# Seven-product block pairs of a fused attention and two-MLP kernel: the next pair's operands made in place, and results turned by VectorE

## The chip, the cores and the metric

The kernel runs on one core of one Trainium2 chip. The metric is the device time of one execution in microseconds; before the change it was 1601.54 us, the median of 3 runs (1599.88 to 1603.52).

## The reference

```python
q_s = softmax(q, axis=-1); k_s = softmax(k, axis=2)      # 8 batches, 8 heads, 576 x 64
kv = einsum('bhsd,bhse->bhde', k_s, v)
x = einsum('bhsd,bhde->bhse', q_s, kv)                   # then 4608 tokens x 512
h = x @ w_in;   x = (h * clip(h + 3, 0, 6) / 6) @ w_out  # first MLP, 512 -> 2048 -> 512
h = x @ w2_in;  out = (h * sigmoid(h)) @ w2_out          # second MLP, same sizes
```

All of it is float32, and the output is 4608 x 512. The softmaxes subtract the largest value and add 1e-9 to the sum.

## The kernel before, in words

The 4608 tokens are 9 blocks of 512. Within the program activations lie transposed: a tile has 128 features on the partitions and 512 tokens along the free dimension. Every float32 product is made of three passes of TensorE over rounded halves, high x high, high x low and low x high, so each operand is kept as a high part (a rounding copy on ScalarE) and a low part (a subtraction on VectorE).

`first_block` and `middle` do the attention and the first MLP of blocks 0 to 6, up to about 725 us. `second_mlp` (line 1315) does the rest in five passes and a tail. A pass (`PASSES`, line 56) takes two neighbouring blocks j and j + 1 of one MLP: (second MLP, 1 and 2), (first MLP, 7 and 8), then the second MLP of 3 and 4, 5 and 6, 7 and 8. The tail does the second MLP of block 0 in the ordinary way, hidden block by hidden block.

In a pass the product of the weight's four quarters with the pair's four quarters is made of seven products in place of eight (Winograd's form): sums of quarters of the weights (A11, S1, ...) lie ready in DRAM (`ws`), sums of the pair's quarters (B11, B21, B22, T1 to T4; the dictionary `op`) lie in SBUF, each with a high and a low half and two chunks c. The first half of a pass (`inner`, line 1337, into the hidden layer) has 8 groups of 7 products, the second (`outer`, line 1508, out of the hidden layer) 7 products of 8 steps. A product is 6 matmuls of 128x512. In the first half ScalarE, VectorE and GpSimd join the products and apply the gate (`pair_events`, line 1373); in the second they split the gated tiles, `LOOK` = 4 products ahead (`split`, `split_low`, lines 1449 to 1455), into one of five buffers (`split_tile`), and join the results into the eight tiles `fixed` (`joins`, line 1522).

The order is written by hand: `when(t, fn)` puts a piece of work at time t, counted in products, and the program is issued in the order of t. Each engine then runs its own instructions in that order and waits at the head of its queue for whatever it needs. SP issues all transfers of the passes. Among them are the weights: a ring of six entries, each two slots of `ws` and 512 KB (`fetch`, line 1190); an entry is fetched again as soon as TensorE has read it.

Two pieces of that order concern the change:

- *The next pair's operands* (`x_ahead`, line 1466). In the first half of a pass, four raw tiles per chunk c are loaded, GpSimd makes the differences (`total`), ScalarE the high parts (`high`) and VectorE the low parts (`low`). They go into buffers of `split_tile` and from there to a DRAM tensor `xd`, since the operands' own tiles `op` are still being read by this half. In the second half `x_fetch` (line 1505) brings them back from `xd` into `op`.
- *The results of a second-MLP pass* (`turn`, line 1553). `fixed` holds them transposed. Eight times per pass TensorE transposes four 128x128 blocks into a PSUM bank, ScalarE copies the bank into a small tile, and SP stores it, 256 KB in rows of 2 KB. For passes 1, 3 and 4 this lies in the first half of the pass that follows, for the last pass in the first eight hidden blocks of the tail.

Of the kernel before, what the change touches and what calls it, by code (L numbers as in the profile page):

```python
# [18 lines left out]
P = 128  # L19
# [9 lines left out]
def efficient_attention_then_two_mlps(  # L29
# [54 lines left out]
    xd = dram.tile([7, P, 2, 2, BLK], F32, name="xd")  # L84
# [1230 lines left out]
    def second_mlp(last):  # L1315
# [148 lines left out]
        XS = ("B11", "T2", "T1", "B21", "T3", "B22", "T4")  # L1464

        def x_ahead(b, c, t, step):

            ph, j = PASSES[b]
            st, hl = {}, {}

            def load(n):
                if n in ("B22", "B21"):
                    pair = gs.tile([P, 2, BLK], F32, tag="g", name="xst")
                    st[n], st[{"B22": "B12", "B21": "B11"}[n]] = pair[:, 0], pair[:, 1]
                jj, h = int(n[2] == "2"), int(n[1] == "2")
                nc.sync.dma_start(st[n], yd[j + jj, 2 * h + c] if ph else xq[j + jj - FAR, 2 * h + c])

            def high(n, src):
                hl[n] = split_tile(True)
                nc.scalar.copy(hl[n][0], st[src])  # L1480

            def low(n, src):
                hi, lo = hl.pop(n)
                add(lo, st[src], f32(hi), ALU.subtract)
                to = xd[XS.index(n)]
                nc.sync.dma_start(to[:, 0, c], f32(hi))
                nc.sync.dma_start(to[:, 1, c], f32(lo))
# [16 lines left out]

        def x_fetch(n, low):
            nc.sync.dma_start(f32(op[n][low]), xd[XS.index(n)][:, low])

# [14 lines left out]
        def joins(b, p, t):  # L1522

            def do(m, name):
                one, two, three, four = fixed[4 * m : 4 * m + 4]
                at = d[b, p][m]
                if name in ("s1", "s5", "C11"):
                    nc.scalar.copy({"s1": one, "s5": three, "C11": four}[name], at)
                elif name == "U2":
                    add(two, at, one)  # L1530
                elif name == "U3":
                    d[b, "U3", m] = small("U3")
                    add(d[b, "U3", m], at, one)
                elif name == "C22":
                    add(three, d.pop((b, "U3", m)), three)
                elif name == "C12":
                    add(two, at, two)
                else:
                    add(one, at, one)
# [13 lines left out]
        def turn(j, k, bank=bank):  # L1553

            h, i = (1, k) if k < NCH else (0, k - NCH)
            at = bank()
            for a in range(2):
                for m in range(2):
                    x = fixed[4 * m + ((3, 1), (0, 2))[a][h]]
                    c = 2 * a + m  # L1560
                    nc.tensor.transpose(  # L1561
                        at[:, c * P : (c + 1) * P], x[:, i * P : (i + 1) * P], ident
                    )
            o = small("o2")
            nc.scalar.copy(o, at)
            rows = out[(j + h) * BLK : (j + h + 1) * BLK, :].rearrange("(p i) d -> i p d", i=NCH)
            nc.sync.dma_start(rows[i], o)
# [4 lines left out]
        for b, (ph, j) in enumerate(PASSES):  # L1572
# [35 lines left out]
            if b + 1 < BB:  # L1608
                x_ahead(b + 1, 0, t0 + (7.0 if b else 9.5), 3.0 if b else 2.8)
                x_ahead(b + 1, 1, t0 + 28.0, 3.0)  # L1610
                for m, n in enumerate(XS):
                    for low in range(2):
                        when(
                            start[0] + 3.1 + 6.0 * m + 3.0 * low,
                            lambda n=n, low=low: x_fetch(n, low),
                        )
                for k in range(2 * NCH if ph else 0):
                    when(T + 3.95 + 5.0 * k, lambda j=j, k=k: turn(j, k))
# [23 lines left out]
        for f in range(NF):  # L1642
            s = (1, 0, f)
            mm1(s)
            if f < 2 * NCH:
                turn(PASSES[-1][1], f, a_pool)
# [63 lines left out]
```

## Time and profile before

| what | value |
|---|---|
| runs, median (lowest to highest) | 1601.54 us (1599.88 to 1603.52) |
| profiled execution: own time; span of its instructions | 1602.64 us; 1600.9 us |
| TensorE busy | 1573.0 us, 98% |
| VectorE, ScalarE, GpSimd busy | 1119.9 us (70%), 788.7 us (49%), 473.6 us (30%) |
| granted TensorE clock, mean | 0.998 of full speed |
| DMA | 401.60 MB, mean 251 GB/s, SP's queue 75.1% of the engines' time |

PE is TensorE's matmuls, PEld its weight loads, which run beside them; DVE is VectorE, ACT ScalarE, POOL GpSimd, SP the engine that issues transfers. A row of the chain gives start, length and work; a row of a timeline adds the idle time before the work and what ended it. The rows sit in the section before the prediction.

### The profile page before, as it was taken

What the parts mean: (1) busy time and instruction counts of PE and PEld (TensorE: products, weight loads), DVE (VectorE), ACT (ScalarE), POOL (GpSimd) and SP (SyncE); (2) the same over time, 40 slices, a digit from 0 to 9 for tenths busy, and PEclk for the clock granted to TensorE, in tenths of its full rate; (3) what the DMA queues carried; (4) which work ended last, traced back from release to release, by engine and by line L of the source; (5) the groups of instructions that cost most, each with busy time, mean ns of one, the idle gap of its engine ahead of it and who ended that gap; (6) DMA issues with size and microseconds to landing.
All of it is one profiled execution on the core that took longest, in us unless ns stands there. A gap on an engine that the chain in (4) does not pass through costs nothing.

```text
span 1600.9 us, 23136 instructions
## 1 busy us (share of the span) xinstructions
PE 1573.0 (98%) x7516; PEld 1287.1 (80%) x7516; DVE 1119.9 (70%) x1856; ACT 788.7 (49%) x1422; POOL 473.6 (30%) x443
## 2 busy tenths in 40 slices
PE   5999999999999999999999999999999999999998
PEld 3778888887878888887888888888888888888887
DVE  8898577777767777676877667668757775567522
ACT  5787345455555554454554445444535553445322
POOL 3334133335333334542410451045005500330000
PEclk9999999999999999999999999999999999999999
DMA  9814976777777776758988898898979896669730
GB/s 274 322 37 151 323 200 200 219 219 223 234 218 207 227 232 187 244 171 315 351 298 286 298 349 300 316 318 311 330 255 330 321 330 237 214 227 358 246 126 27
DMA packets 352424, 401.60 MB, mean 251 GB/s; under 512 B 120496, under 2 KB 233136, under 8 KB 352304
## 3 DMA queue, kind: packets, MB, share of 16 engines
q1 hardware_dynamic: 350256, 399.05, 75.1%
q8 instruction: 60, 0.98, 0.3%
q10 hardware_dynamic: 2048, 1.08, 0.2%
q14 instruction: 60, 0.49, 0.1%
HBM read 276.56 MB, written 123.47 MB: 250 GB/s over the span
## 4 chain that ended last, share of the span: by engine, by line
PE 90%; DVE 4%; DMA 3%; ACT 1%; issue 1%; SPq 0%; POOL 0%; ACTq 0%; DVEq 0%; POOLq 0%
PE pb L1516 24%; PE pb L1346 22%; PE h L562 20%; PE y L634 17%; PE y L636 3%; PE pa L516 2%; PE pa L398 1%; PE pb L1561 1%; DVE fa L140 1%; DMA xst<-yd 0%; DVE fa L144 0%; DMA xst<-xq 0%; DVE h L599 0%; DMA yd<-o 0%; DMA ring<-ws 0%
## 5 line engine op out<-in xcount | busy, mean ns | idle before, releaser
L1346 PE MATMUL pb<-xo,ring 128*128 128x512 f32 x1680 | 391.3, 391 | 1.2 <-ACT s L1386 0.9
L562 PE MATMUL h<-x,wi 128*128 128x512 f32 x1536 | 382.8, 396 | 1.8 <-ACT g L610 1.4
L1516 PE MATMUL pb<-gsp,ring 128*128 128x512 f32 x1680 | 382.4, 389 | 0.0
L1516 PEld LDWEIGHTS pb<-gsp,ring 128*128 128x128 f32 x1680 | 315.3, 188 | 65.5
L1346 PEld LDWEIGHTS pb<-xo,ring 128*128 128x128 f32 x1680 | 313.1, 188 | 68.0 <-ACT s L1386 2.9
L562 PEld LDWEIGHTS h<-x,wi 128*128 128x128 f32 x1536 | 285.4, 190 | 63.9 <-ACT g L610 2.2
L634 PE MATMUL y<-g,wo 128*128 128x512 f32 x1344 | 324.6, 391 | 1.1 <-DVE o L653 1.1
L634 PEld LDWEIGHTS y<-g,wo 128*128 128x128 f32 x1344 | 251.1, 188 | 54.1 <-DVE o L653 1.6
L1333 DVE TENSOR_TENSOR gsp<-g,gsp 128x512 fp32r<-128x512 f32 x240 | 171.8, 722 | 72.6 <-ACT gsp L1451 69.4
L1451 ACT CAST gsp<-g 128x512 fp32r<-128x512 f32 x240 | 144.3, 622 | 139.8 <-DVE gsp L1333 70.8
L1333 POOL TENSOR_TENSOR s<-U,s 128x512 f32<-128x512 f32 x32 | 44.3, 1383 | 384.9 <-DVE U L1333 369.4
L575 ACT ACTIVATE r<-h 128x512 f32<-128x512 f32 x112 | 67.0, 598 | 168.0 <-PE h L562 166.3
L599 DVE SCALAR_TENSOR_TENSOR h<-r,h 128x512 f32<-128x512 f32 x112 | 77.5, 692 | 80.4 <-ACT r L575 79.8
L1333 DVE TENSOR_TENSOR g<-r,pb 128x512 f32<-128x512 f32 x96 | 65.5, 683 | 47.9 <-ACT r L1360 47.7
L1360 ACT ACTIVATE r<-pb 128x512 f32<-128x512 f32 x96 | 57.2, 595 | 70.3 <-DVE pb L1333 59.6
L590 ACT CAST g<-h 128x512 fp32r<-128x512 f32 x112 | 65.6, 585 | 48.5 <-DVE h L599 40.8
L437 POOL TENSOR_TENSOR qe<-qraw,qm 128x512 f32<-128x512 f32 x34 | 39.8, 1170 | 153.5 <-DVE qz L479 144.5
L1333 POOL TENSOR_TENSOR g<-g 128x512 f32<-128x512 f32 x40 | 55.3, 1383 | 91.7 <-DVE g L1333 79.8
L593 DVE TENSOR_TENSOR g<-h,g 128x512 fp32r<-128x512 f32 x96 | 66.0, 687 | 20.5 <-ACT g L590 19.0
L195 POOL TENSOR_TENSOR fa<-fa 128x256 f32<-128x256 f32 x64 | 49.6, 774 | 56.8 <-DVE sp L227 48.0
L1333 DVE TENSOR_TENSOR U<-pb,s 128x512 f32<-128x512 f32 x80 | 54.7, 684 | 13.4 <-PE pb L1346 8.4
L1333 DVE TENSOR_TENSOR gsp<-xst,gsp 128x512 fp32r<-128x512 f32 x56 | 54.0, 965 | 12.7 <-ACT gsp L1480 10.9
(167 smaller groups left out, 1829.7 us busy)
## 6 DMA issues: line engine op xcount, KB each, us to landing
ring<-ws SPq DMA_DIRECT2D x280, 512.0 KB, 5.1
ws<-sp SPq DMA_DIRECT2D x256, 128.0 KB, 2.2
xd<-gsp SPq DMA_DIRECT2D x112, 256.0 KB, 5.5
xo<-xd SPq DMA_DIRECT2D x56, 512.0 KB, 6.3
wi_early<-in_moe_w_in_dram SPq DMA_DIRECT2D x16, 512.0 KB, 8.6
wo_early<-in_moe_w_out_dram SPq DMA_DIRECT2D x16, 512.0 KB, 8.8
wi_raw<-in_moe_w_in_dram SPq DMA_DIRECT2D x16, 512.0 KB, 4.8
ws<-w_sum SPq DMA_DIRECT2D x64, 128.0 KB, 2.1
```

The costliest lines, as they stand in the source:

```text
L195: lambda to=to, x=x, y=y, op=op: nc.gpsimd.tensor_tensor(out=at[to], in0=at[x], in1=at[y], op=op)
L562: nc.tensor.matmul(h, w[:, a, c, :], x[:, e, c, :], start=(c == 0 and n == 0), stop=(c == NC - 1 and n == 2),)
L575: nc.scalar.activation(self.r, self.h, AF.Relu, bias=3.0)
L590: nc.scalar.copy(self.g[:, 0], self.r)
L593: nc.vector.tensor_tensor(out=self.g[:, 1], in0=self.r, in1=f32(self.g[:, 0]), op=ALU.subtract)
L599: nc.vector.scalar_tensor_tensor(out=self.h, in0=self.r, scalar=6.0, in1=self.h, op0=ALU.min, op1=ALU.mult)
L634: nc.tensor.matmul(y[c], w[:, a, cs], g[:, e, :], start=st, stop=sp)
L1333: (eng or nc.vector).tensor_tensor(out=out, in0=a, in1=b, op=how)
L1346: nc.tensor.matmul(to, ws_[:, a], e[:, c], start=p in ("P1", "P6", "P5") and c == 0 and m == 0, stop=c == 1 and m == 2, skip_group_check=True,
L1360: nc.scalar.activation(r, d[b, n, key], AF.Sigmoid)
L1451: nc.scalar.copy(t[0], source(p, i))
L1516: nc.tensor.matmul(d[b, p][m], w[:, a, m * P : (m + 1) * P], t[e], start=new and i == 0 and k == 0, stop=i == NPR - 1 and k == 2, skip_gro ...
```

## The change

The scratch tensor `xd` and `x_fetch` are removed. `x_ahead` now runs in the second half of a pass, when the operands' tiles are no longer read, for chunk 0 from slot 6 and for chunk 1 from slot 30 of the half, and writes `op` directly; its raw tiles come from the pool of small tiles. The joins' tile U3 moves to another pool. `turn` is replaced: VectorE's transpose turns 32x32 blocks within a 128x512 tile, and the rest of the transposition is left to the store, four transfers of 64 KB for each tile, in runs of 32 elements (128 B). In the passes these transfers are 1.3 slots apart (`turn_blocks`), in the tail together (`turn_last`).

```diff
-    xd = dram.tile([7, P, 2, 2, BLK], F32, name="xd")
...
             def load(n):
-                if n in ("B22", "B21"):
-                    pair = gs.tile([P, 2, BLK], F32, tag="g", name="xst")
-                    st[n], st[{"B22": "B12", "B21": "B11"}[n]] = pair[:, 0], pair[:, 1]
+                st[n] = small("xst")
...
             def high(n, src):
-                hl[n] = split_tile(True)
-                nc.scalar.copy(hl[n][0], st[src])
+                nc.scalar.copy(op[n][0][:, c], st[src])

             def low(n, src):
-                hi, lo = hl.pop(n)
-                add(lo, st[src], f32(hi), ALU.subtract)
-                to = xd[XS.index(n)]
-                nc.sync.dma_start(to[:, 0, c], f32(hi))
-                nc.sync.dma_start(to[:, 1, c], f32(lo))
+                hi, lo = op[n]
+                add(lo[:, c], st[src], f32(hi[:, c]), ALU.subtract)
...
-        def x_fetch(n, low):
-            nc.sync.dma_start(f32(op[n][low]), xd[XS.index(n)][:, low])
...
-                    d[b, "U3", m] = small("U3")
+                    d[b, "U3", m] = att.tile([P, BLK], F32, tag="q", bufs=2, name="U3")
...
-        def turn(j, k, bank=bank):
-
-            h, i = (1, k) if k < NCH else (0, k - NCH)
-            at = bank()
-            for a in range(2):
-                for m in range(2):
-                    x = fixed[4 * m + ((3, 1), (0, 2))[a][h]]
-                    c = 2 * a + m
-                    nc.tensor.transpose(
-                        at[:, c * P : (c + 1) * P], x[:, i * P : (i + 1) * P], ident
-                    )
-            o = small("o2")
-            nc.scalar.copy(o, at)
-            rows = out[(j + h) * BLK : (j + h + 1) * BLK, :].rearrange("(p i) d -> i p d", i=NCH)
-            nc.sync.dma_start(rows[i], o)
+        turned = []
+
+        def turn_blocks(j, k, part):
+            h, n = (1, k) if k < NC else (0, k - NC)
+            a, m = divmod(n, 2)
+            x = fixed[4 * m + ((3, 1), (0, 2))[a][h]]
+            if part == 0:
+                if not turned:
+                    turned.extend(split_tile())
+                nc.vector.transpose(f32(turned[0]), x)
+            o = f32(turned[0])
+            rows = out[(j + h) * BLK : (j + h + 1) * BLK, n * P : (n + 1) * P]
+            e = slice(part * 32, part * 32 + 32)
+            nc.sync.dma_start(
+                rows[:, e].rearrange("(b r i) c -> r i b c", b=4, i=NCH),
+                o[e].rearrange("r (i b c) -> r i b c", i=NCH, b=4),
+            )
+            if part == 3:
+                turned.pop(0)
+
+        gone = []
+
+        def turn_last(j, k):
...
+            o = gone.pop() if k else small("o2")
+            gone.append(x)
+            nc.vector.transpose(o, x)
...
             if b + 1 < BB:
-                x_ahead(b + 1, 0, t0 + (7.0 if b else 9.5), 3.0 if b else 2.8)
-                x_ahead(b + 1, 1, t0 + 28.0, 3.0)
-                for m, n in enumerate(XS):
-                    for low in range(2):
+                for c in range(2):
+                    x_ahead(b + 1, c, start[0] + (6.0, 30.0)[c], 3.0)
+                for k in range(2 * NCH if ph else 0):
+                    for i in range(4):
                         when(
-                            start[0] + 3.1 + 6.0 * m + 3.0 * low,
-                            lambda n=n, low=low: x_fetch(n, low),
+                            T + 3.95 + 5.8 * k + 1.3 * i,
+                            lambda j=j, k=k, i=i: turn_blocks(j, k, i),
                         )
-                for k in range(2 * NCH if ph else 0):
-                    when(T + 3.95 + 5.0 * k, lambda j=j, k=k: turn(j, k))
...
             if f < 2 * NCH:
-                turn(PASSES[-1][1], f, a_pool)
+                turn_last(PASSES[-1][1], f)
```

VectorE's order moves in the second half of a pass. Here is a piece of the second pass's second half before; `gsp<-g` and `gsp<-spare` are low parts for the products, `g_...<-spare` sums of gated tiles:

```order
L1333 TENSOR_TENSOR gsp<-g_8265,gsp 128x512
L1333 TENSOR_TENSOR gsp<-g_8350,gsp 128x512
L1333 TENSOR_TENSOR gsp<-spare,gsp 128x512
L1333 TENSOR_TENSOR g_7896<-spare,g_7896 128x512
L1333 TENSOR_TENSOR gsp<-spare,gsp 128x512 x2
L1333 TENSOR_TENSOR g_7992<-spare,g_7992 128x512
L1333 TENSOR_TENSOR gsp<-spare,gsp 128x512 x3
L1333 TENSOR_TENSOR g_8087<-spare,g_8087 128x512
```

And the same piece with the change; `xo<-xst` is a low part of an operand of the next pair, made from the raw tile `xst`:

```order
L1332 TENSOR_TENSOR gsp<-g_8249,gsp 128x512
L1332 TENSOR_TENSOR xo<-xst,xo 128x512
L1332 TENSOR_TENSOR gsp<-spare,gsp 128x512
L1332 TENSOR_TENSOR g_7866<-spare,g_7866 128x512
L1332 TENSOR_TENSOR gsp<-spare,gsp 128x512 x2
L1332 TENSOR_TENSOR xo<-xst,xo 128x512
L1332 TENSOR_TENSOR g_7941<-spare,g_7941 128x512
L1332 TENSOR_TENSOR gsp<-spare,gsp 128x512 x3
L1332 TENSOR_TENSOR xo<-xst,xo 128x512
L1332 TENSOR_TENSOR g_8017<-spare,g_8017 128x512
```

The subtractions for the operands now stand between the sums and the low parts for the products, one for about every three products.

SP's order moves in the first half of a pass. Here is a piece of the fourth pass's first half before: raw tiles, weight fetches, the stores to `xd` and one store of a result among them:

```order
L1476 DMA xst<-yd 128x512 x4
L1567 DMA out_dram<-o_11695 128x512
L1193 DMA ring<-ws 128x2x512 x2
L1486 DMA xd<-gsp 128x512
L1487 DMA xd<-gsp 128x512
L1193 DMA ring<-ws 128x2x512
L1567 DMA out_dram<-o_11764 128x512
L1193 DMA ring<-ws 128x2x512
L1486 DMA xd<-gsp 128x512
L1487 DMA xd<-gsp 128x512
```

And with the change, from the third pass's second half into the fourth's first:

```order
L1471 DMA xst<-yd 128x512 x4
L1192 DMA ring<-ws 128x2x512 x17
L1556 DMA out_dram<-gsp 128x4x32
L1192 DMA ring<-ws 128x2x512
L1556 DMA out_dram<-gsp 128x4x32
L1192 DMA ring<-ws 128x2x512
L1556 DMA out_dram<-gsp 128x4x32 x2
L1192 DMA ring<-ws 128x2x512
L1556 DMA out_dram<-gsp 128x4x32
```

The raw tiles are now loaded in the second half, and the first half's queue holds weight fetches and the short stores alone.

TensorE's order loses the transposes. In the fourth pass's first half it had:

```order
L1346 MATMUL pb<-xo,ring 128x512 x30
L1561 MATMUL pb<-ident,vbuf 128x128
L1561 MATMUL pb<-ident,fin 128x128
L1561 MATMUL pb<-ident,kbuf_101 128x128
L1561 MATMUL pb<-ident,fin 128x128
L1346 MATMUL pb<-xo,ring 128x512 x30
```

With the change that half, with the second half before it and the products that lead over into its own, reads:

```order
L1345 MATMUL pb<-xo,ring 128x512 x6
L1504 MATMUL pb<-gsp,ring 128x512 x330
L1345 MATMUL pb<-xo,ring 128x512 x330
L1504 MATMUL pb<-gsp,ring 128x512 x6
L1345 MATMUL pb<-xo,ring 128x512 x6
```

Nothing stands between the products any more.

## Rows read from the trace of the kernel before

**Rows 1.** The page: busy time, share of the span and instructions of each engine.
```profile
PE 1573.0 (98%) x7516; PEld 1287.1 (80%) x7516; DVE 1119.9 (70%) x1856; ACT 788.7 (49%) x1422; POOL 473.6 (30%) x443
```

**Rows 2.** Waits of PE, 720 to 1510 us: who waited for whom; total, times, longest.
```profile
PE pb L1346 <- ACT s L1386: 0.9, 1, 0.9
PE pb L1346 <- DVE U L1333: 0.2, 1, 0.2
```

**Rows 3.** Busy time by stretch: first half, second half, last pass's first half.
```profile
core 0: us, PE busy (x) PEld busy (x) DVE busy (x) ACT busy (x) POOL busy (x), PEclk, DMA share, GB/s
...
1193.10:1269.60 76.50, 76.50 (x354) 63.20 (x353) 53.85 (x74) 36.25 (x68) 39.87 (x29) 1.00 0.94 331
1274.60:1349.40 74.80, 74.80 (x332) 61.94 (x331) 53.28 (x82) 35.12 (x61) 3.30 (x2) 1.00 0.83 295
1349.40:1425.80 76.40, 76.40 (x354) 63.12 (x353) 40.29 (x60) 29.67 (x54) 27.14 (x21) 1.00 0.64 209
```

**Rows 4.** The chain that ended last: first half, second half, tail; start, us, what.
```profile
1199.03 6.86 PE pb L1346 x30
...
1206.32 6.86 PE pb L1346 x30
...
1274.61 74.80 PE pb L1516 x330
...
1514.83 2.72 PE h L562 x12
...
1520.76 2.72 PE h L562 x12
```

**Rows 5.** DMA issues: out<-in, queue, op, count, KB each, median us to landing.
```profile
ring<-ws SPq DMA_DIRECT2D x280, 512.0 KB, 5.1
...
xd<-gsp SPq DMA_DIRECT2D x112, 256.0 KB, 5.5
xo<-xd SPq DMA_DIRECT2D x56, 512.0 KB, 6.3
...
out_dram<-o SPq DMA_DIRECT2D x32, 256.0 KB, 3.7
```

**Rows 6.** Busy time by stretch: the tail, after its last turn.
```profile
1555.00:1590.00 35.00, 35.00 (x156) 28.97 (x155) 8.97 (x13) 7.47 (x13) 0.00 (x0) 1.00 0.06 20
```

**Rows 7.** The chain that ended last, in the first pass's first half.
```profile
740.70 6.83 DMA xst<-xq
...
755.76 0.48 ACT s L1386
```

**Rows 8.** Groups of instructions: line, engine, op, shapes, count; busy us, mean ns; idle before.
```profile
L1333 DVE TENSOR_TENSOR gsp<-xst,gsp 128x512 fp32r<-128x512 f32 x56 | 54.0, 965 | 12.7 <-ACT gsp L1480 10.9 <-DMA xd<-gsp 0.9 <-DMA ring<-ws 0.9
...
L1480 ACT CAST gsp<-xst 128x512 fp32r<-128x512 f32 x56 | 35.0, 626 | 9.8 <-issue 3.0 <-DMA xst<-xq 2.9 <-DMA xst<-yd 2.7
...
L479 DVE STREAM_TRANSPOSE qz<-qe 128x512 f32<-128x512 f32 x27 | 19.0, 705 | 2.2 <-POOL qe L463 0.9 <-DMA yd<-o 0.6 <-DMA ws<-fa 0.5
```

**Rows 9.** Timeline of DVE in the third pass's second half.
```profile
1159.84 0.69 DVE L1333 TENSOR_TENSOR gsp<-g,gsp 128x512 fp32r<-128x512 f32 x1
...
1174.05 0.69 DVE L1333 TENSOR_TENSOR g<-g,spare 128x512 f32<-128x512 f32 x1
1174.65 0.69 DVE L1333 TENSOR_TENSOR kbuf<-U,kbuf 128x512 f32<-128x512 f32 x1
```

**Rows 10.** Timeline of DVE in the fourth pass's first half, GpSimd busy beside it.
```profile
1217.03 1.52 DVE L1333 TENSOR_TENSOR gsp<-xst,gsp 128x512 fp32r<-128x512 f32 x1
```

**Rows 11.** Timeline of ACT in the third pass's second half.
```profile
1159.18 0.62 ACT L1451 CAST gsp<-g 128x512 fp32r<-128x512 f32 x1 [0.74 <-DVE gsp L1333]
```

**Rows 12.** The q loads' issues on SP: duration ns min/median/max, first and last start.
```profile
L489 SPq DMA_DIRECT2D qt<-zd x108: 557/635/1460, 200.7 to 692.1; - x108
```

**Rows 13.** Timeline of SP in the third pass's second half.
```profile
1122.46 0.36 SPq L1193 DMA_DIRECT2D ring<-ws  x1
...
1125.18 3.08 SPq L1193 DMA_DIRECT2D ring<-ws  x2
```

**Rows 14.** Busy time by stretch: two us in which q loads (issued 310.8 to 313.5) move.
```profile
313.00:315.00 2.00, 2.00 (x11) 1.65 (x10) 1.12 (x4) 0.52 (x2) 1.04 (x1) 1.00 0.63 99
```

More of the change, by code (lines that the diff above doesn't have):

```diff
@@ L1462, in next_t4 @@
             add(g_of(2 * i)[:, 1], g_of(2 * i + 1)[:, 0], op["spare"][:, i], ALU.subtract)
-        XS = ("B11", "T2", "T1", "B21", "T3", "B22", "T4")
         def x_ahead(b, c, t, step):
             ph, j = PASSES[b]
-            st, hl = {}, {}
+            st = {}
             def load(n):
-                if n in ("B22", "B21"):
-                    pair = gs.tile([P, 2, BLK], F32, tag="g", name="xst")
-                    st[n], st[{"B22": "B12", "B21": "B11"}[n]] = pair[:, 0], pair[:, 1]
+                st[n] = small("xst")
                 jj, h = int(n[2] == "2"), int(n[1] == "2")
@@ L1551, in joins @@
                 when(t + k, lambda m=m, name=name: do(m, name))
-        def turn(j, k, bank=bank):
-            h, i = (1, k) if k < NCH else (0, k - NCH)
-            at = bank()
-            for a in range(2):
-                for m in range(2):
-                    x = fixed[4 * m + ((3, 1), (0, 2))[a][h]]
-                    c = 2 * a + m
-                    nc.tensor.transpose(
-                        at[:, c * P : (c + 1) * P], x[:, i * P : (i + 1) * P], ident
-                    )
-            o = small("o2")
-            nc.scalar.copy(o, at)
-            rows = out[(j + h) * BLK : (j + h + 1) * BLK, :].rearrange("(p i) d -> i p d", i=NCH)
-            nc.sync.dma_start(rows[i], o)
+        turned = []
[18 more added lines that the diff above has]
+        def turn_last(j, k):
+            h, n = (1, k) if k < NC else (0, k - NC)
+            a, m = divmod(n, 2)
+            x = fixed[4 * m + ((3, 1), (0, 2))[a][h]]
+            o = gone.pop() if k else small("o2")
+            gone.append(x)
+            nc.vector.transpose(o, x)
+            rows = out[(j + h) * BLK : (j + h + 1) * BLK, n * P : (n + 1) * P]
+            for i in range(4):
+                e = slice(i * 32, i * 32 + 32)
+                nc.sync.dma_start(
+                    rows[:, e].rearrange("(b r i) c -> r i b c", b=4, i=NCH),
+                    o[e].rearrange("r (i b c) -> r i b c", i=NCH, b=4),
+                )
         T = 0.0
@@ L1608, in second_mlp @@
             if b + 1 < BB:
-                x_ahead(b + 1, 0, t0 + (7.0 if b else 9.5), 3.0 if b else 2.8)
-                x_ahead(b + 1, 1, t0 + 28.0, 3.0)
-                for m, n in enumerate(XS):
-                    for low in range(2):
+                for c in range(2):
+                    x_ahead(b + 1, c, start[0] + (6.0, 30.0)[c], 3.0)
+                for k in range(2 * NCH if ph else 0):
+                    for i in range(4):
                         when(
-                            start[0] + 3.1 + 6.0 * m + 3.0 * low,
-                            lambda n=n, low=low: x_fetch(n, low),
-                        )
-                for k in range(2 * NCH if ph else 0):
-                    when(T + 3.95 + 5.0 * k, lambda j=j, k=k: turn(j, k))
+                            T + 3.95 + 5.8 * k + 1.3 * i,
+                            lambda j=j, k=k, i=i: turn_blocks(j, k, i),
+                        )
             else:
```

## Prediction

> **What bounds the kernel now.** I began with the shares of busy time: TensorE is busy for 1573.0 of a 1600.9 us span, VectorE for 1119.9, ScalarE for 788.7 [rows 1]. So time goes where TensorE's instructions go, unless something makes it wait. The waits of TensorE over the five passes say that nearly nothing does: 0.9 us and 0.2 us in some 780 us [rows 2]. The table by stretches shows it stage by stage: in a first half with turns, in a second half, and in the first half of the last pass PE is busy for the whole stretch, 76.50 of 76.50, 74.80 of 74.80 and 76.40 of 76.40 us, at a granted clock of 1.00, that is 2.4 GHz [rows 3]. What the change does to VectorE, GpSimd or the transfers is therefore worth nothing by itself; it counts what it takes from PE's queue, and it costs what it makes PE wait.
>
> **What it takes from PE.** The chain of waits gives the price of a turn. In the second half 330 matmuls take 74.80 us, so one takes 0.2267 us and thirty take 6.80. In the first half thirty matmuls and one turn take 1206.32 - 1199.03 = 7.29 us: a turn (four transposes) costs 0.49 us of PE's time. In the tail twenty-four matmuls and a turn take 1520.76 - 1514.83 = 5.93 us, against 24 x 0.2267 = 5.44: again 0.49 [rows 4]. There are 32 turns, one for each store of a result of 256 KB [rows 5]. The change removes them all: 32 x 0.49 = **15.7 us**. Does PE then run on through the gaps? In the tail from the ninth hidden block on there is no turn already, and there PE is busy for 35.00 of 35.00 us [rows 6]; in the first half of the last pass, after its turns, it is the same [rows 3]. So the turns cover nothing that would show up.
>
> **The wait that goes with them.** The 0.9 us wait is for a copy of line 1386, and the chain has that copy at 755.76 us, in the first pass's first half. Ahead of it the chain holds a transfer of 6.83 us that brings raw operands of the next pair [rows 7]: ScalarE's queue stood behind it, and the gate of the hidden layer behind that. This work leaves the first half. Between 0 and 1.1 us come back; I take 0.9, the whole of that wait, since the cause is gone.
>
> **What moves into the second half.** Per pass but the last, 14 splits of the next pair's operands: a copy on ScalarE (626 ns) and a subtraction on VectorE (965 ns on average, 56 of each in all) [rows 8]. Their 112 stores of 256 KB and the 56 loads of 512 KB go altogether [rows 5], each a place in SP's queue ahead of the weights. The second half leaves DVE 74.80 - 53.28 = 21.5 us and ACT 39.7 us of idle time [rows 3]; 14 x 0.965 = 13.5 us and 14 x 0.626 = 8.8 us fit as a sum. But both queues run in order, so I also count where they are densest. Instructions of DVE follow each other at 0.60 us (1174.65 - 1174.05) [rows 9]. Between the slots 29.7 and 50 of the half (20.3 products of six matmuls, 1.36 us each, 27.6 us) DVE gets 20 splits of products, 8 sums of gated tiles, 7 splits of operands and 6 joins: 41 x 0.60 = 24.6 us. Four GpSimd subtractions fall there too; beside one, a subtraction of VectorE took 1.52 us in place of 0.69 [rows 10], so up to 4 x 0.8 = 3.2 us more: 27.8, as much as there is. What covers the excess is the look-ahead: the copy for a product is made four products early (5.44 us), and copy and subtraction are over 1.35 us after the copy's start [rows 9, 11], so 4.1 us are in hand. Lower bound 0; upper bound, with every DVE instruction at its listed 0.69 us and the lows at 1.52: 34 x 0.69 + 7 x 1.52 = 34.1 us, 6.5 over, 2.4 beyond what is in hand, in each of four halves: 9.6 us. I take **0**, since the 0.60 is read in that very half. The raw operands must land before the first copy, 4.3 slots or 5.8 us after their issue; the slowest landing shown is 6.83 [rows 7], a delay of 1 us, inside the 4.1. On SP the loads stand between weight fetches and wait only for buffers last used in the first half or 4 slots earlier.
>
> **What the turns become.** On VectorE 32 transposes of 128x512. The one transpose that the trace shows took 705 ns [rows 8]; 24 of them fall in first halves, where 14 of the 965 ns subtractions leave and 8 transposes come, so DVE there gets lighter: 53.85 - 13.5 + 8 x 0.71 = 46 of 76.5 us [rows 3, 8]. Cost 0; with GpSimd beside each, 8 x 0.8 = 6.4 us of DVE time, still less than leaves. ScalarE loses 24 + 8 copies. On SP four stores follow each transpose: 128 in all, each 64 KB in 512 runs of 128 B. The nearest issue is that of the q loads, also 64 KB in such runs: 0.635 us [rows 12]. With 28 weight fetches of 0.36 us, SP issues for 32 x 0.635 + 28 x 0.36 = 30 of 76 us. SP waits for a transpose before its first store, and behind that stands a weight fetch. Fetches have room: one follows another at 2.72 us, the ring holds six, so five intervals (13.6 us) pass before use, of which landing takes 5.1 [rows 5, 13]: 8.5 us in hand.
>
> **The transfers themselves** are the open price; no store in short runs to DRAM is in the trace. The q loads' reads are the nearest: about 2 us behind their issue (the usual landing is 2.7) the 16 DMA engines were busy for 0.63 of the time at 99 GB/s [rows 14], which is 48 runs of 128 B per us and engine, 13 ns each. A store then takes 32 x 13 = 0.42 us of each engine, and stores come every 1.3 slots, 1.77 us: share 0.24. The weights' share is that of the last pass's first half, 0.64 at 209 GB/s, less its eight stores: 0.56 [rows 3]. Together 0.80: no queue grows. From the other side, a 2 KB run costs 0.83 of a us for 9 runs per engine, 92 ns [rows 3]; at that price the stores alone would take 94 us of a half of 76. I take 13 ns, the same run length. The Trainium skill ("DMA: Bandwidth & Descriptors", Specifications) states that below 512 B the DMA does a read-modify-write. Taken as twice the price of a run, that would make the share 1.04 and the last store some 2 us late, inside the 8.5 us in hand, and the time 1585 as well; only a costlier round trip for each run leads to rival 2, on whose side the rule stands. No run here shows it yet.
>
> **The sum.** The profiled execution took 1602.64 us, 1.7 beyond its span. 1602.64 - 15.7 - 0.9 = 1586.0. It stood 1.1 above the median of the runs, 1601.54, so the median should come to **1585.0**.
>
> **Rivals.**
> 1. *The second half starves* (0.06). A copy of an operand stands at the head of ScalarE's queue until its transfer or GpSimd's subtraction is there, and copies for the products wait behind it. It decides once a delay passes 4.1 us. Against it: a slowest landing of 6.83 us; for it: DVE's densest 27 us hold 27.8 us of work. If each of four halves loses 3.5 us: 1585 + 14 = 1599, the gain given back.
> 2. *The short stores clog the DMA queues* (0.07), and weight fetches, which share those queues, come late. Every 1.77 us the engines owe 0.99 to the weights; a run at 24 ns fills the rest, and from 38 ns on (15 us late by the last store, less the 8.5 in hand, in three halves) the gain is lost. At four times the read's price, 52 ns: 32 x 0.88 = 28 us late, 20 us of stall in each of three halves: 1585 + 58 = 1643, **slower**. Against it: the reads at 13 ns, a third of the price that decides. For it: a store is not a read, no row shows one, and the bounds reach from 13 to 92 ns.
> 3. *The first half's gate comes late* (0.04): a transpose beside GpSimd sits ahead of a gate's multiplication and holds a PSUM bank. At 2 us in each of three halves: 1591. Against it: VectorE's queue there loses more than it gets.
> 4. *The turns were covered* (0.03): PE then waits where they stood, and the time stays at 1601. Against it: [rows 6].
>
> **Chances and range.** The forecast has 0.80, with a spread of 1581 to 1589 (a single run of before differs from its median by up to 2 us, and the wait's and the second half's bounds are inside). Rival 3 lies within 1592; left out are rivals 1, 2 and 4, together 0.16: range 1581 to 1592. 0.2% is 3.2 us, about what a measurement tells from no change. Faster by more than that: 0.80 + 0.04 and half of rival 1, 0.87; within: the other half and rival 4, 0.06; slower: 0.07.
>
> **What would show it.** Right: no transpose left in PE's list but those of the attention; first halves of the passes all 76.2 us long (336 matmuls); PE's waits over the passes under 1 us; the second halves at 74.8 with DVE near 66 us busy; the store's landing under 4 us, weight fetches still near 5. Wrong: a PE wait for DVE or ACT on gsp in second halves (rival 1), a PE wait for the ring with a DMA share near 1 in the second, fourth and fifth first halves (rival 2), PE waits for g or banks there (rival 3).

## The result, and the profile after

| | before | after |
|---|---|---|
| runs, median (lowest to highest) | 1600.71 us (1599.39 to 1603.52), 4 runs | 1584.31 us (1583.04 to 1585.70), 4 runs |
| ratio after to before, 95% interval | | 0.9895 [0.9878, 0.9913] |
| profiled execution: own time; span | 1602.64 us; 1600.9 us | 1584.67 us; 1583.0 us |

The kernel is faster by 16.4 us; 1585.0 had been forecast. (The median of before is here over four runs, one more than at the time of the prediction.)

The page's busy times, against [rows 1]: PE has 128 matmul records fewer, the four transposes of each of 32 turns, and 17.7 us less work. VectorE has more to do, ScalarE less.

```profile
PE 1555.3 (98%) x7388; PEld 1274.9 (81%) x7388; DVE 1146.3 (72%) x1888; ACT 775.1 (49%) x1390; POOL 490.8 (31%) x443
```

The table of PE's waits between 720 and 1510 us, which had two entries [rows 2], is empty. The chain that ended last is a chain of matmuls alone there (start, us, what); the pieces left out are like these:

```profile
726.28 2.73 PE pb L1345 x12
...
806.54 74.80 PE pb L1504 x330
881.34 74.80 PE pb L1345 x330
...
958.86 74.80 PE pb L1504 x330
...
1490.62 5.44 PE h L561 x24
```

Every half but the very first, which begins among the last products of the stage before, is now 330 matmuls in 74.80 us, with 2.72 us for the twelve that lead over from a first half into a second; the second halves had this length already [rows 4]. The stretches (columns as in [rows 3]) show what lies beside it. In order: a first half with stores, one without, the fourth pass's second half with the new work in it (the three passes before have DVE at 66.47 to 67.08 us there), and 40 us of the densest stores.

```profile
881.30:956.10 74.80, 74.80 (x332) 61.94 (x331) 46.81 (x71) 27.27 (x49) 27.11 (x21) 1.00 0.81 219
1033.70:1108.50 74.80, 74.80 (x331) 61.94 (x330) 42.21 (x63) 27.27 (x49) 27.11 (x21) 1.00 0.60 198
...
1263.50:1338.30 74.80, 74.80 (x331) 61.94 (x331) 66.41 (x95) 42.05 (x75) 21.82 (x10) 1.00 0.66 225
900.00:940.00 40.00, 40.00 (x178) 33.14 (x177) 25.88 (x40) 14.83 (x27) 15.52 (x13) 1.00 0.86 231
```

PE is busy for all of every stretch at a granted clock of 1.00. DVE stands at 66.41 us of 74.80 in the second half, where it had 53.28. The 32 stores of a first half raise the DMA share from 0.60 to 0.81: 0.21 x 74.8 us for 1024 runs of 128 B per engine, 15 ns a run.

The list of DMA issues (out<-in, queue, count, KB each, median us to landing) answers to [rows 5]: over the whole run weight fetches land sooner than before (5.1), the short stores of the passes in 4.0 us.

```profile
ring<-ws SPq DMA_DIRECT2D x280, 512.0 KB, 3.9
...
out_dram<-gsp SPq DMA_DIRECT2D x96, 64.0 KB, 4.0
```

Their issue on SP takes what the q loads' did [rows 12] (view of one line: duration ns min/median/max, first and last start):

```profile
L1556 SPq DMA_DIRECT2D out_dram<-gsp x96: 596/597/1478, 885.5 to 1404.0; - x96
```

Three groups of instructions of after (columns as in [rows 8]). The moved subtraction has become shorter, 681 ns for 965. GpSimd's differences, which were 1382 ns on average in the first halves, have become longer. The transposes cost what the one of [rows 8] did.

```profile
L1332 DVE TENSOR_TENSOR xo<-xst,xo 128x512 fp32r<-128x512 f32 x56 | 38.1, 681 | 5.2 <-ACT xo L1474 4.6 <-DMA ring<-ws 0.3
...
L1552 DVE STREAM_TRANSPOSE gsp<-fin 128x512 f32<-128x512 f32 x12 | 8.5, 704 | 0.0
...
L1332 POOL TENSOR_TENSOR xst<-xst 128x512 f32<-128x512 f32 x32 | 71.5, 2235 | 167.5 <-DVE xo L1332 87.1 <-DMA xst<-yd 46.4 <-DMA xst<-xq 17.3
```

### The profile page after: what moved, and what is told of

Read it like the earlier page. It is cut to its first block, busy times and chain, and to the rows that moved or that the text cites. A ratio compares the mean times of both kernels' runs of the same rounds, so it can differ in the third digit from the quotient of the medians.

```text
span 1583.0 us, 22655 instructions
## 1 busy us (share of the span) xinstructions
PE 1555.3 (98%) x7388; PEld 1274.9 (81%) x7388; DVE 1146.3 (72%) x1888; ACT 775.1 (49%) x1390; POOL 490.8 (31%) x443
## 4 chain that ended last, share of the span: by engine, by line
PE 93%; DVE 3%; DMA 1%; ACT 1%; issue 1%; SPq 0%; POOL 0%; ACTq 0%; DVEq 0%; POOLq 0%
PE pb L1345 24%; PE pb L1504 24%; PE h L561 21%; PE y L633 17%; PE y L635 3%; PE pa L515 2%; PE pa L397 1%; DVE fa L139 1%; DMA yd<-o 0%; DVE fa L143 0%; DVE fa L132 0%; DVE h L598 0%; DMA wi_early<-in_moe_w_in_dram 0%; DMA ws<-fa 0%; PE pa L368 0%
## 5 line engine op out<-in xcount | busy, mean ns | idle before, releaser
L1345 PE MATMUL pb<-xo,ring 128*128 128x512 f32 x1680 | 382.6, 389 | 0.0
L1332 DVE TENSOR_TENSOR gsp<-g,gsp 128x512 fp32r<-128x512 f32 x240 | 182.5, 780 | 25.4 <-ACT gsp L1450 24.7
L1332 POOL TENSOR_TENSOR xst<-xst 128x512 f32<-128x512 f32 x32 | 71.5, 2235 | 167.5 <-DVE xo L1332 87.1
```

What stands on the lines that cost most here:

```text
L1332: (eng or nc.vector).tensor_tensor(out=out, in0=a, in1=b, op=how)
L1345: nc.tensor.matmul(to, ws_[:, a], e[:, c], start=p in ("P1", "P6", "P5") and c == 0 and m == 0, stop=c == 1 and m == 2, skip_group_check=True,
```

## The experiments

Eleven kernels ran, in three groups, each group on one chip together with the kernel before; ratios are to that kernel in the same group (medians 1601.33, 1600.28 and 1600.48 us). The theory is that of the prediction: only what leaves PE's queue counts, the rest is covered. The rivals are the second half that starves (1) and the short stores that delay the weights (2).

### The two parts alone

**In place only.** The change, with the turns as they were (TensorE, a copy on ScalarE, one store of 256 KB):

```diff
-                    for i in range(4):
-                        when(T + 3.95 + 5.8 * k + 1.3 * i,
-                            lambda j=j, k=k, i=i: turn_blocks(j, k, i))
+                    when(T + 3.95 + 5.0 * k, lambda j=j, k=k: turn(j, k))
```

> The kernel with the change, but results are turned as before (TensorE, ScalarE copy, 256 KB stores); only the next pair's operands are made in place in the second half. Theory (the gain is PE's time for 32 turns, 15.7 us, plus the two stalls of the first halves of passes 1 and 2, 1.8 + 0.9 us by the lengths of those halves in the two traces): about 2.7 us less than before, 1598, with no PE wait in the passes. Rival (the turns were covered and the traffic through DRAM was what cost): most of the gain, about 1585 to 1588.

Measured: 1599.19 us (11 runs), ratio 0.9988 [0.9979, 0.9997], so 0.5 to 3.4 us are gained. The chain of this kernel has the turns (L1549) in line between the matmuls, at thirty matmuls in 6.86 us and a turn in 0.44, as before [rows 4]:

```profile
887.36 6.86 PE pb L1345 x30
894.21 0.44 PE pb L1549 x4
894.65 6.86 PE pb L1345 x30
```

The move of the operands is worth some 2 us, by the stalls that are gone, and the remaining 15 us are the turns'.

**Turning only.** The kernel before, operands by `xd`, with VectorE's transposes and the short stores:

```diff
-        def turn(j, k, bank=bank):
+        def turn_blocks(j, k, part):
...
-                for k in range(2 * NCH if ph else 0):
-                    when(T + 3.95 + 5.0 * k, lambda j=j, k=k: turn(j, k))
+                for k in range(2 * NCH if ph else 0):
+                    for i in range(4):
+                        when(T + 3.95 + 5.8 * k + 1.3 * i,
+                            lambda j=j, k=k, i=i: turn_blocks(j, k, i))
```

> The kernel before, with VectorE's transposes and the short stores (turned into the pool of small tiles), but the operands still made in the first half and sent through DRAM. Theory: the 15.7 us of the turns go, the stalls of the first halves stay or grow, since in two of the three first halves with turns the DMA engines were busy for 0.93 of the time and the short stores add 0.21 less 0.08: 1585 if the 8.5 us in hand of the weights cover it, up to 1592 with PE waiting for the ring. Rival (turns covered): 1600. Rival (the two parts are independent and DMA has room): 1585 with the ring landing within 6 us.

Measured: 1593.03 us (5 runs), ratio 0.9949 [0.9937, 0.9962]; 1 us above the upper end of what was expected, and only half of the turns' 15.7 us is gained. PE does not wait for the ring, as the theory had it: its waits over the passes are in the first halves' line, for DVE's joins and for copies of the gates:

```profile
PE pb L1346 <- DVE U L1333: 2.8, 3, 0.9
PE pb L1346 <- ACT s L1386: 2.4, 4, 1.1
```

So the parts don't add up: 2 and 8 us alone, 16 together. Three more kernels take this one apart.

### Where turning alone loses its gain

All three keep the operands on the way by `xd`; their edits are shown against turning only. The first has the stores in runs of 2 KB, one of 256 KB per tile, as the turns of before had them (which part of the output a store holds is then not the reference's):

```diff
-            rows = out[(j + h) * BLK : (j + h + 1) * BLK, n * P : (n + 1) * P]
-            e = slice(part * 32, part * 32 + 32)
-            nc.sync.dma_start(
-                rows[:, e].rearrange("(b r i) c -> r i b c", b=4, i=NCH),
-                o[e].rearrange("r (i b c) -> r i b c", i=NCH, b=4),
-            )
+            rows = out[(j + h) * BLK : (j + h + 1) * BLK, :].rearrange("(p i) d -> i p d", i=NCH)
+            if part == 0:
+                nc.sync.dma_start(rows[n], o)
```

> As the run with VectorE's transposes alone (operands still through DRAM), but in the passes each transposed tile leaves in one store of 256 KB in runs of 2 KB in place of four short ones; the output of the passes is not put together, its 32x32 blocks stay unplaced. That run lost 5.2 and 2.6 us in the two first halves that have both turns and operands. Theory A (the short stores: with them the DMA engines' share there was 1.03, and SP's queue is fuller): the losses go back to about 0.9 and 0, time about 1586. Theory B (VectorE's transposes stand ahead of the gate and hold it): the losses stay, 1593.

The second has the transposes and no stores in the passes, the third neither:

```diff
-            nc.sync.dma_start(
-                rows[:, e].rearrange("(b r i) c -> r i b c", b=4, i=NCH),
-                o[e].rearrange("r (i b c) -> r i b c", i=NCH, b=4),
-            )
```

> As the last, but VectorE does transpose the 24 tiles of the passes; only their stores are left out (so these results are missing from the output). If the transposes in VectorE's queue delay the gates: above the kernel without them by 1 us or more, near 1589, what the kernel with stores in 2 KB runs took. If the stores alone are at fault: as the kernel without them.

```diff
-                for k in range(2 * NCH if ph else 0):
+                for k in range(0):
                     for i in range(4):
                         when(T + 3.95 + 5.8 * k + 1.3 * i,
```

> The kernel before, its operands still by DRAM, with the 24 results of the passes neither turned nor stored (they are left out of the output), and the tail's eight turned by VectorE. Question: where does the turning-only kernel lose its 8.5 us. Theory A (what is added in the first halves, transposes and short stores, delays them): without them nothing is late, all first halves are 77.5 us apart from their start to the next, about 1585. Theory B (the turns were PE's slack: with them gone the gates of a first half, behind the splits of the next pair in ScalarE's and VectorE's queues, come late whatever is stored): halves with the next pair's splits still lose 2 us and more each, 1588 to 1592.

| added in the first halves | median (lowest to highest) | ratio, 95% interval |
|---|---|---|
| nothing | 1584.70 us (1583.82 to 1585.11) | 0.9900 [0.9885, 0.9914] |
| transposes | 1587.24 us (1586.32 to 1588.55) | 0.9919 [0.9902, 0.9935] |
| transposes, stores in 2 KB runs | 1589.01 us (1585.96 to 1591.69) | 0.9929 [0.9910, 0.9949] |
| transposes, stores in 128 B runs | 1593.03 us (1591.86 to 1596.10) | 0.9949 [0.9937, 0.9962] |

The same stretch, the second pass's first half, in the four kernels (columns as in [rows 3]). Neither transposes nor stores:

```profile
880.00:957.00 77.00, 77.00 (x341) 63.75 (x341) 55.10 (x78) 33.94 (x63) 41.04 (x29) 1.00 0.92 317
```

Transposes:

```profile
880.00:957.00 77.00, 76.87 (x340) 63.37 (x339) 58.23 (x83) 33.33 (x63) 40.95 (x29) 1.00 0.91 314
```

Transposes and stores in 2 KB runs:

```profile
880.00:957.00 77.00, 76.46 (x333) 61.95 (x333) 54.51 (x80) 30.19 (x56) 37.89 (x27) 1.00 0.93 330
```

Transposes and stores in 128 B runs:

```profile
880.00:957.00 77.00, 75.73 (x330) 61.33 (x330) 54.85 (x80) 30.16 (x56) 40.80 (x29) 1.00 1.03 323
```

PE's busy time falls step by step, and in the last the DMA share passes 1. Theory B of the kernel without transposes and stores falls: with the turns simply gone, the first halves carry the making of the operands nearly without a loss (PE's waits over the passes are 0.6 us in all). The loss comes from what replaces the turns, on VectorE and in the transfers, on top of the operands' splits and their way to `xd` and back. Turning only has a half that shows this too: the last pass's first half has the same transposes and stores and makes no operands, and it runs at full pace, while those of the second and fourth pass are 5.2 and 2.6 us longer.

```profile
1346.75 74.80 PE pb L1346 x330
```

With the operands moved away, the change has the same transposes and stores in a half with DVE at 46.81 us and a share of 0.81, and loses nothing. The transposes alone cost 2.5 us, as the first alternative of their run had it: no run with them was as short as the longest without, in one group of runs. What the stores add on top is less sure: the kernel with 2 KB runs lies between its two theories, its runs spread over 6 us and its profile is of the longest. Neighbouring steps of the table have overlapping intervals (and the last two rows come from other groups of runs than the first two); the first and the last don't overlap.

One more thing differs between turning only and the change, and no run separates it. In turning only a transposed tile lies in the pool of small tiles, from which the joins and gates take theirs, until its four stores have landed; in the change it lies in a buffer of `split_tile`, which the operands have left free. Two waits for such a landing stand in the trace of turning only, 720 to 1510 us:

```profile
POOL s L1333 <- DMA out_dram<-o: 3.5, 1, 3.5
...
ACT r L1360 <- DMA out_dram<-o: 2.9, 1, 2.9
```

How much of the 8 us is VectorE's queue, the transfers or these buffers stays open.

### The short stores

**Twice.** In the change, each short store is followed by another of the same runs, into a scratch tensor:

```diff
+            more = o[part * 32 : part * 32 + 32]
+            nc.sync.dma_start(sd[j, k, part][:, :, 0:32], more.rearrange("r (q c) -> r q c", c=32))
```

> The changed kernel with every short store of the passes issued a second time into a scratch tensor, so twice the 128 B runs and twice the issues. By the trace after, 32 stores raise the DMA share of a first half from 0.60 to 0.81, 15 ns for a run; where the stores stand (62 us) that is 0.88, and twice is 1.15. Theory: a queue of up to 9 us grows by the end, the ring's landing doubles to 8 us or more, and the 9.7 us that the weights have in hand about cover it: 1584 to 1590. Rival (short stores are free to the weights): 1584.3 with the ring landing at 3.9. Rival (already on the edge): over 1595.

Measured: 1583.67 us, ratio 0.9889 [0.9876, 0.9903], no wait of PE in the passes. Over the whole run weights landed in 4.0 us (3.9 in the change), but most of the 280 fetches have no short store beside them. For those issued from 885 to 945 us, in the second pass's first half, the two rows below give the change and then this kernel: 4.3 and 4.9 us, where the change has 3.6 in the half without stores (1040 to 1100 us). So the short stores do make the weights later, but by far less than the doubling of the theory, and what is in hand covers it. The time is that of the first rival, whose landing of 3.9 us does not hold beside the stores. The third row is this kernel's densest stretch, with a DMA share of 1.00 where the change had 0.86.

```profile
ring<-ws SPq DMA_DIRECT2D x22, 512.0 KB, 4.3
```

```profile
ring<-ws SPq DMA_DIRECT2D x21, 512.0 KB, 4.9
```

```profile
900.00:940.00 40.00, 40.00 (x179) 33.10 (x178) 25.66 (x39) 14.65 (x27) 16.11 (x13) 1.00 1.00 240
```

**Three times.** The second store takes 64 partitions, 1024 runs (its line in the rows below is L1562, the first store's L1557):

```diff
+            more = o[(part % 2) * 64 : (part % 2) * 64 + 64]
+            nc.sync.dma_start(sd[j, k, part][:, :, 0:32], more.rearrange("r (q c) -> r q c", c=32))
```

> The changed kernel with three times the short runs of the passes (for each store a second one of 64 partitions, 1024 runs of 128 B, into a scratch tensor). With twice the runs the dense stretch of a first half showed a DMA share of 1.00, the ring still landed in 4.0 us and the time was the same. Theory (the share is a measure of occupancy and not of queueing, but it has an end): now runs wait, the ring's landing grows to 6 us or more; the weights have 9.7 us in hand, so 1584 to 1595. Rival (short runs are as good as free to the weights): ring at 4, 1584. Rival 2 of the prediction (queue grows without end): over 1600.

Measured: 1611.84 us, ratio 1.0072 [1.0054, 1.009]: slower than before. Of what was expected, only the last rival has such a time, and the cause is not the one that it names. PE waits for weights:

```profile
PE pb L1346 <- DMA ring<-ws: 10.1, 12, 1.6
PE pb L1505 <- DMA ring<-ws: 8.5, 3, 3.9
```

These waits are 18.6 of the 27.5 us by which the run is longer than the change; part of the rest is that after a wait the matmuls ran below the full clock (a mean granted clock of 0.66 from 960 to 970 us). Yet a fetch issued from 885 to 945 us lands 5.0 us after its issue (median), hardly later than with twice the runs:

```profile
ring<-ws SPq DMA_DIRECT2D x18, 512.0 KB, 5.0
```

It is the issue that is late, as SP's timeline in a first half shows (start, us, what): the additional store takes up to 2.35 us to issue (0.67 at the median), the fetch behind it comes that much later, and SP has no pause between one transfer and the next.

```profile
900.49 0.68 SPq L1557 DMA_DIRECT2D out_dram<-gsp  x1
901.22 2.35 SPq L1562 DMA_DIRECT2D sd<-gsp  x1
903.67 1.04 SPq L1193 DMA_DIRECT2D ring<-ws  x1
```

Rival 2 exists, then, with its edge between twice and three times the runs, and it acts through SP's queue and not through the landing. With twice the runs SP was nearly as full there, with as many issues, the longest of the additional store 1.57 us; the DMA share over 885 to 945 us was 0.95 there and is 1.03 here. Why an issue becomes so long is not shown.

**Bunched.** The change's "spread" undone, the four stores of a tile in a row:

```diff
-                            T + 3.95 + 5.8 * k + 1.3 * i,
+                            T + 3.95 + 5.8 * k,
```

> The changed kernel with the four stores of a result issued in a row in place of 1.3 slots apart. Theory (SP's queue and the DMA engines have room): a weight fetch behind them comes up to 1.8 us later, of 9.7 in hand: the same time, 1584. Rival (spreading them is what keeps PE fed): PE waits of a us or more per result, 24 of them: over 1600.

Measured: 1583.52 us, ratio 0.9896 [0.988, 0.9911]. The stores land sooner (2.3 us for 4.0), the weights as in the change (3.8 us for 3.9); the spreading is worth nothing here.

```profile
out_dram<-gsp SPq DMA_DIRECT2D x96, 64.0 KB, 2.3
```

### The second half

**Look-ahead of two products in place of four.**

```diff
-    LOOK = 4
+    LOOK = 2
```

> The changed kernel with the look-ahead of the second half cut from 4 products to 2, 2.7 us less in hand. In the trace after, the least that a low part was early before its product was about 1.5 us, of 4.1 at rest. Theory (the moved work is covered by the look-ahead, and most of it is used): PE waits in the four second halves with operands, about 1.2 to 2.5 us each, 1589 to 1594, and none in the last pass's. Rival (the moved work fits without it): 1584.3.

Measured: 1589.62 us, ratio 0.9928 [0.9913, 0.9943]. The time is as expected and the place is not: each of the five second halves, the last one without new work too, loses 1 to 1.5 us at its start. The chain at the starts of the second and the last:

```profile
963.49 1.20 DVE gsp L1332
...
964.73 70.82 PE pb L1504 x311
...
1424.24 1.20 DVE gsp L1332
1425.48 70.83 PE pb L1504 x311
```

There the last gate of the first half and the splits of the first products come together. From there on the 311 matmuls take 70.82 us against 311 x 0.2267 = 70.50 at full pace, with or without the new work. So this run did not show what the operands' splits need of the look-ahead; it showed that the hand-over needs it.

**The lows twice.** Each low part of the next pair's operands is subtracted twice, 14 more instructions of VectorE in each of four second halves:

```diff
-                add(lo[:, c], st[src], f32(hi[:, c]), ALU.subtract)
+                for _ in range(2):
+                    add(lo[:, c], st[src], f32(hi[:, c]), ALU.subtract)
```

> The changed kernel with each low part of the next pair's operands subtracted twice, 14 more VectorE instructions in each of four second halves. There DVE was busy for 66.8 of 74.8 us; 14 x 0.60 more are 75.2. Theory (the second half holds the moved work only just): the densest 27.6 us get 32 us of work, of which at most 1.5 to 2 us can be taken from the look-ahead that is left: PE waits for gsp, 2 to 4 us in each of four halves, 1592 to 1600. Rival (DVE has idle time enough, the queue shifts): 1584.3.

Measured: 1609.10 us, ratio 1.0054 [1.0036, 1.0072], beyond the expectation and slower than before. The wait of PE is the one that rival 1 names:

```profile
PE pb L1505 <- DVE gsp L1332: 15.2, 16, 2.1
```

The chain of the fourth pass's second half (start, us, what) leaves PE at 1300.35 us and stays on VectorE, but for one copy of 0.63 us and short gaps between instructions, until 1347.40:

```profile
1281.28 19.05 PE pb L1505 x84
...
1300.35 0.69 DVE gsp L1332
...
1345.67 1.68 DVE gsp L1332
...
1347.40 15.28 PE pb L1505 x59
1362.68 2.49 PE pb L1345 x11
```

The half takes 1362.68 - 1281.28 = 81.40 us in place of 74.80: 14 x 0.60 = 8.4 us of additional work cost 6.6. Not all of that is waiting for VectorE: the last 59 matmuls, after the last wait, took 15.28 us, against 59 x 0.2267 = 13.38 at full pace. In that stretch the mean granted clock was 0.89, after PE had waited 1.2 and 2.1 us, where it was 1.00 up to there:

```profile
1347.40:1362.68 15.28, 15.28 (x60) 12.47 (x61) 10.99 (x18) 2.53 (x5) 0.00 (x0) 0.89 0.42 145
```

So 1.9 us are the clock's and 4.7 are VectorE's lateness. Of 8.4 us of additional work the half took in 8.4 - 4.7 = 3.7, out of VectorE's pauses and the look-ahead together; that much room was left beside the moved work.

**GpSimd's differences on VectorE.**

```diff
-                add(st[to], st[x], st[y], ALU.subtract, nc.gpsimd)
+                add(st[to], st[x], st[y], ALU.subtract)
```

> The change, with the differences of raw tiles (eight per pair) on VectorE instead of GpSimd. Theory: GpSimd's subtraction of 7.09 us in a second half was covered by the look-ahead, and VectorE's 8 more instructions of 0.6 us per half (4.8 us) are fewer than the 14 that cost 6 us a half in the run with doubled subtractions; subtractions of VectorE are also no longer slowed by GpSimd beside them: 1584, no PE waits. Rival: the second half is at its edge already, and 4.8 us more of VectorE's work lose 2 us in each of four halves: 1592.

Measured: 1583.89 us, ratio 0.9895 [0.988, 0.991], no wait of PE. The same stretch as above, 1263.50 to 1338.30, has more instructions of DVE (105 for 95) in less busy time (64.78 for 66.41 us), and almost nothing on GpSimd:

```profile
1263.50:1338.30 74.80, 74.80 (x332) 61.96 (x331) 64.78 (x105) 42.24 (x75) 3.31 (x2) 1.00 0.67 225
```

So additional instructions are not all alike: those that replace work of GpSimd give VectorE back what its neighbour had cost.

## Why the prediction was right, point by point

- **The turns, 15.7 us: right.** The halves with turns fell to 74.80 us as all others. In the profiled executions the passes take 778.90 and 764.34 us, the tail up to the last matmul is 3.95 shorter (8 turns of 0.49). (The spans differ by 17.9: 0.5 more is gained before the passes, and 1.1 lost after the last matmul.) The kernel that leaves the passes' turns out, has VectorE turn the tail's and moves no operands took 1584.70 against 1600.48, 15.8 less; that the turns were covered (rival 4) is excluded.
- **The stall, 0.9 us: mis-sized in the profiled executions.** "I take 0.9, the whole of that wait, since the cause is gone." In the two profiled executions 14.56 us go in the passes, of which 24 turns x 0.49 are 11.8; 2.7 are left, three times the term. The first pass's first half gives 1.8 of them and the second's 0.9. The table of PE's waits listed 1.1 in all; the lengths of the halves would have shown more. The lines of before, from the chain:

```profile
726.78 2.73 PE pb L1346 x12
...
808.83 74.80 PE pb L1516 x330
...
966.03 74.80 PE pb L1516 x330
...
1505.68 2.72 PE h L562 x12
```

  The first pass's first half took 808.83 - 726.78 = 82.05 us, and 806.54 - 726.28 = 80.26 with the change. Whether it is as much in a typical run stays open: in-place alone gained 0.5 to 3.4 us, and the medians differ by 16.4, which leaves 0.7 to the stall. If it was 2.7, it is by luck that the sum came so near.
- **The second half, 0: right.** DVE came to 66.41 us where 66 was forecast, and PE never waited. The sum for the densest stretch, as much work as time, was nearly right too: in the fourth pass VectorE has the 41 instructions that were counted and is busy for 25.76 of 27.60 us there (1303.90 to 1331.50), with one pause of 1.84. With 8.4 us more, the half became VectorE's. Rival 1 was a true mechanism, some 4 us of additional VectorE work away. The "4.1 us in hand" were tested by neither run: the shorter look-ahead failed elsewhere, and the 3.7 us of the doubled subtractions hold VectorE's pauses too.
- **Transposes and stores, 0: right, but only beside the other part.** "DVE there gets lighter" was the reason, and it was a needed one: with the operands still made in the first half the same transposes and stores cost 8 us, by VectorE's queue, the transfers or the buffers. The prediction costed the two parts as if each kept its value alone; it said nothing of what turning alone would bring.
- **A store's run, 13 ns taken: 15 measured.** The forecast share of 0.80 was for where the stores stand, and there it is 0.86 (weights 0.60 for 0.56, stores 0.26 for 0.24). The Trainium skill ("DMA: Bandwidth & Descriptors", Specifications) states a read-modify-write below 512 B; at 15 ns for a written run beside 13 for a read one, no doubling shows here. Rival 2 put its edge at 38 ns, 2.9 times the read's price, on a longer landing; the runs put it between two and three times the runs, at SP's queue. (Two sums of that rival are slightly off: 32 x (32 x 0.038 + 0.99 - 1.77) is 14 us and not 15, and three stalls of 20 are 60 and not 58.)
- **Gates (rival 3): not seen** in the change, where PE's table of waits is empty. It is what happens in turning only, whose waits are for `s` and `U`.
- **The signs.** Two came out otherwise: the short stores landed in 4.0 us, where under 4 was named, and the weights in 3.9, where near 5 was named. The weights' landing was taken from a kernel whose `xd` traffic the change removes.
- **The sum.** 1585.0 against 1584.31, within what two sets of runs of one kernel differ by.

## What to carry to other kernels

When one engine is busy for 98% of the time at full clock, count first the instructions that leave its queue: 32 turns at 0.49 us gave nearly the whole result, and everything else was worth 0 to 3 us. Work that goes to another engine instead needs room there, stage by stage; two moves that look separate, out of a half and into it, can be worth 2 and 8 us alone and 16 together, because one makes the room the other needs. A median over a whole run can hide what happens beside the new work; ask for the stretch. And where a cover is said to hide work, find its end by doubling the work: here twice the stores were free and three times were not, and twice the subtractions cost more than the whole change had gained.

## What the runs showed of the hardware

- A GpSimd subtraction of 128x512 that takes 1.6 us in the same half took 7.09 while VectorE ran without a pause beside it; VectorE's own instructions kept their 0.60 us pace there. VectorE waited at the end of it for the copy that needed the result. The timeline of GpSimd and then of VectorE in after:

```profile
1308.76 1.62 POOL L1332 TENSOR_TENSOR xst<-xst 128x512 f32<-128x512 f32 x1 [2.49 <-issue]
1321.24 7.09 POOL L1332 TENSOR_TENSOR xst<-xst 128x512 f32<-128x512 f32 x1 [10.86 <-DVE xo L1332]
```

```profile
1323.49 0.68 DVE L1332 TENSOR_TENSOR g<-g,spare 128x512 f32<-128x512 f32 x1
1324.09 0.68 DVE L1332 TENSOR_TENSOR gsp<-g,gsp 128x512 fp32r<-128x512 f32 x1
...
1329.02 0.69 DVE L1332 TENSOR_TENSOR xo<-xst,xo 128x512 fp32r<-128x512 f32 x1 [1.84 <-ACT xo L1474]
```

  It cost nothing: with that work on VectorE the time was the same.
- Beside 128 B stores the weights landed in 4.3 us (3.6 in a half without them), in 4.9 with twice the stores at a DMA share of up to 1.00, in 5.0 with three times the runs. What gave first, at three times, was the issue on SP: up to 2.35 us for a transfer that takes 0.62 at its shortest.
- Twice the runs raised the share in the 40 us from 0.86 to 1.00, and not by the 0.26 that the first ones had added to the 0.60 of a half without them; the share is no measure of how many more fit.
- After waits of 1.2 and 2.1 us TensorE ran 59 matmuls at a mean granted clock of 0.89, between its two levels of 1.2 and 2.4 GHz, and took 1.9 us longer for them than at full pace (the run with doubled subtractions).
